# PSUM banks of nine Q blocks, the place of PQ's scaling, and the place and bank of gb's ones matmul

## Chip, core and metric

The kernel runs on one core of a Trainium2 chip. Times are device microseconds (us) of one launch. Most launches of one kernel agree within some tenths of a per cent (six of before lie within 840.26 to 841.36 us, 0.13%); every comparison of times is made with launches of the same rounds on the same chip. A profile is one such launch. The rounds ran on different chips (the medians of before were 840.96 us on chip 10, 840.87 on chip 2 and 840.8 on chip 6), so figures read from traces are compared across chips.

Five engines work side by side: TensorE (PE: matmuls; PEld: its weight loads), VectorE (DVE), ScalarE (ACT), GpSimd (POOL) and the DMA queue that SyncE (SP) feeds (in before PE was busy for 831.1, PEld for 383.5, DVE for 511.4, ACT for 336.3 and POOL for 36.3 us of the same 839.8). Matmul results go to PSUM, of which this kernel uses eight banks (0 to 7); its semaphores let a bank be written again only when the last reader is done.

## The reference, cut to what matters

```python
h = layernorm(x) * (1 + ca) + sa
q, k, v = split(h @ wqkv)                  # 2048 rows, 1024 columns, 32 heads
pq, pk = phi(q), phi(k)                    # phi(t) = max(t, 0) + min(exp(t), 1) + 1e-6, in effect
kv, z = sum pk*v, sum pk                   # per head, over all rows
o = (pq @ kv) / (pq @ z + 1e-6)            # "den" is pq @ z
x = x + ga * (o @ wo)
h = layernorm(x) * (1 + cb) + sb
x = x + gb * ((gelu(h @ w_gate) * (h @ w_up)) @ w_down)
# sa, ca, ga, sb, cb, gb: six rows of silu(c) @ w_mod
```

The first stretch that matters lies where k and v are done: the last Q blocks, den, and the fold of kv into wo (W2). The second lies at the end of the FFN of the first quarter of the rows, where the row gb is summed and spread to all partitions.

## The kernel before: the parts that matter

A helper records every operation with what it reads and writes, and turns the overlaps into semaphore waits; each engine then runs its own operations in the order of recording (in before DVE waited 0.79 us for rb, though an evacuation stood behind in its queue). So the order of the calls below is the order in each engine's queue.

A Q block is eight matmuls of 128x512 into one bank, and its evacuation is three instructions: exp on ACT, then two on DVE.

```python
def phi(bank, dst_ap, dst_rng, note):              # L669, L670, L672
    ACT: EB = exp(PS(bank))
    DVE: EB = min(EB, 1) + 1e-6
    DVE: dst = max(PS(bank), 0) + EB               # the last reader of the bank
```

den multiplies PQ with z, and its evacuation and the reciprocal follow on DVE; the reciprocal goes out to memory and comes back, spread over the partitions, as rb (sixteen loads). `pq_scale` multiplies PQ by rb on DVE, in place.

```python
q_todo += [(NSG - 1, qc) for qc in range(NG)]
qn = [0]

def q_next(evac=True):
    sg, qc = q_todo.pop(0)
    b = (0, 1, 2, 0)[qn[0]] if qn[0] < 4 else (qn[0] + 1) % 2
    qn[0] += 1
    q_block(sg, qc, evac, b)
    return sg, qc, b

first_q = q_next(False)
kvacc(NCH - 1)
zcols()
q_evac(*first_q)
q_next()
den(0, 3)                  # 32 small matmuls into bank 3; on DVE: +1e-6, reciprocal; store
rb_load(0)
rb_load(1)
kvbd()                     # DVE: three instructions, reads banks 5 to 7
q_next()
q_next()                   # the fourth Q block
for u in range(NG):
    q_next()
    if u == 0:
        kvt()              # eight transposes into bank 4
    else:
        w2_pair(u - 1)     # two matmuls into banks 2 and 3, copied by ACT
    if u in (2, 3):
        pq_scale(0, 0, GH[u - 2])
    if u in (5, 6):
        pq_scale(0, 1, GH[u - 5])
w2_pair(NG - 1, 4)
```

So the twelve Q blocks go to banks 0, 1, 2, 0, and then 1, 0, 1, 0, 1, 0, 1, 0. I number them from 1.

gb is summed on DVE in the first FFN, split in two bf16 parts (`gb_hi` on ACT, `gb_lo` on DVE), summed over the partitions by four matmuls with a matrix of ones, copied by ACT, stored and loaded back over all partitions:

```python
def gb_rows():
    mod_rows(((0, 2, 6, lambda j, h: (HLG[:, j, h, :], r_hlg(j, h))),))   # 4 matmuls 32x512, bank 6 (L643)
    o_ = mod_store(2, 6, MRG, [...], 2)                                   # ACT copy (L649), store
    row_load(GBB, R_GBB, 2, 0, "gbb", o_)

for fc, fn in ((14, lambda: gb_hi(0)), (16, lambda: gb_lo(0)), (24, lambda: gb_hi(1)), (25, lambda: gb_lo(1)), (26, gb_rows)):
    gb_at.setdefault(fc, []).append(fn)     # called after FFN column block fc of the first group
...                                         # fc runs 0 to 27; then the down projection, banks 6, 7, 4, 5, ...
```

## Time and profile before

| | before |
|---|---|
| time, median of the first 3 launches | 841.0 us (840.83 to 841.36) |
| PE busy | 831.1 of 839.8 us |
| from the third Q block to the first Wo matmul | 22.70 us |
| hole around the ones matmuls of gb | 1.48 us |

The page's first parts. Line one is the span; the PE and DVE lines are busy time, share and number of instructions; PEclk is the granted clock in tenths, in 40 slices.

```profile
span 839.8 us, 11286 instructions
...
PE 831.1 (99%) x4160; PEld 383.5 (46%) x4160; DVE 511.4 (61%) x893; ACT 336.3 (40%) x555; POOL 36.3 (4%) x91
...
PEclk9999999999999999999999999999999999999999
```

Matmuls fill the span, at full clock (mean granted clock 1.000). What can still be gained without taking work away is where PE waits. All its waits, from the view of waits for PE (engine, line, waited for: us in total, times, longest):

```profile
PE ps_all L478 <- DMA c<-in_c_dram: 2.7, 1, 2.7
PE ps_all L600 <- DMA wmq<-in_w_mod_dram: 1.2, 1, 1.2
PE ps_all L721 <- DVE pq L672: 1.1, 2, 0.7
PE ps_all L680 <- DVE h1T L565: 0.6, 2, 0.4
PE ps_all L643 <- DVE hlg L1176: 0.5, 1, 0.5
```

The first, second and fourth belong to the first 27 us and are not touched. The third and the last are the targets. PE's timeline (start, duration, line, operation, in brackets the idle time and what ended it) shows where they lie. First the Q stretch:

```profile
176.18 5.35 PE L721 MATMUL ps_all<-h1T,wq 128*128 128x512 bf16 x24
181.37 0.61 PE L940 MATMUL ps_all<-ident,kvbd 128*128 128x128 bf16 x8
182.72 1.89 PE L721 MATMUL ps_all<-h1T,wq 128*128 128x512 bf16 x8 [0.74 <-DVE pq L672]
...
190.92 0.59 PE L947 MATMUL ps_all<-wo,kvt 128*128 128x512 bf16 x2
191.85 1.90 PE L721 MATMUL ps_all<-h1T,wq 128*128 128x512 bf16 x8 [0.34 <-DVE pq L672]
193.59 0.59 PE L947 MATMUL ps_all<-wo,kvt 128*128 128x512 bf16 x2
194.12 1.90 PE L721 MATMUL ps_all<-h1T,wq 128*128 128x512 bf16 x8
...
198.88 3.62 PE L1045 MATMUL ps_all<-w,pq 128*128 128x512 bf16 x16
```

An entry's duration includes the pipelined tail of its last matmul (one full matmul is recorded with 0.38 us, and the next starts 0.22 after it: 348.03 and 348.25 below), so holes are best measured from starts. A full matmul starts 0.216 us after the one before it (see the FFN lines below), a block of eight 1.73 us after. The transposes of 181.37 are issued by 181.82, and the next block starts at 182.72: 0.9 us of nothing, though the table of waits says 0.74. Two W2 matmuls take 0.43; so 191.85 comes 0.5 us late and 194.12 about 0.1. DVE's timeline shows why:

```profile
177.50 1.75 DVE L965 RECIPROCAL rdc<-rdc 128x256 f32<-128x256 f32 x1
179.17 1.29 DVE L934 TENSOR_TENSOR kvbd<-ps_all,bmask 128x384 bf16<-128x384 f32 x3
...
181.88 0.69 DVE L672 SCALAR_TENSOR_TENSOR pq<-ps_all,eb 128x512 bf16<-128x512 f32 x1
...
189.44 1.29 DVE L991 TENSOR_TENSOR pq<-pq,rb 128x512 bf16<-128x512 bf16 x2 [0.79 <-DMA rb<-scr_rd]
190.65 0.42 DVE L670 TENSOR_SCALAR eb<-eb 128x512 f32<-128x512 f32 x1
191.11 0.69 DVE L672 SCALAR_TENSOR_TENSOR pq<-ps_all,eb 128x512 bf16<-128x512 f32 x1
```

The entry at 181.88 is the last reader of the fourth block's bank 0, and ends at 182.57; it comes late because reciprocal (1.75) and kvbd (1.29) stand ahead of it. The block at 182.72 (the sixth) rewrites bank 0. The entry at 189.44 is the scaling: it waits 0.79 us for rb, and the evacuation at 191.11 stands behind it; the block at 191.85 needs that bank.

Second, the ones matmuls (L643), between FFN column blocks 26 and 27 (L1102 and L1105):

```profile
348.03 0.38 PE L1102 MATMUL ps_all<-h2T,wg 128*128 128x512 bf16 x1
348.25 0.38 PE L1105 MATMUL ps_all<-h2T,wu 128*128 128x512 bf16 x1
348.55 0.60 PE L643 MATMUL ps_all<-hlg,ones 128*32 128x512 bf16 x3
349.62 0.39 PE L643 MATMUL ps_all<-hlg,ones 128*32 128x512 bf16 x1 [0.47 <-DVE hlg L1176]
349.95 0.39 PE L1102 MATMUL ps_all<-h2T,wg 128*128 128x512 bf16 x1
```

PE would go on at 348.25 + 0.216 = 348.47; it goes on with full matmuls at 349.95, after a hole of 1.48 us, in which the fourth ones matmul waits for `gb_lo(1)` on DVE (hlg).

### The profile page before, as it was taken

The numbers are of one execution on the slowest core, as the hardware profiler recorded it, in microseconds if no ns is written. First come the engines' busy times: TensorE is split into PE (matmuls) and PEld (weight loads), VectorE is DVE, ScalarE is ACT, GpSimd is POOL, SyncE is SP. The second block draws the span as 40 slices with busy tenths as digits, with TensorE's granted clock in tenths as the row PEclk, the third lists the DMA queues.
The fourth block names the chain that finished last, engine by engine and source line by source line (L and its number), as shares of the span: only waits on it lengthen the run. The fifth ranks groups of instructions, "written<-read, shape, count | busy, mean of one in ns | idle before, by whom it ended". The sixth has DMA issues, their size and how long they took to land.

```text
span 839.8 us, 11286 instructions
## 1 busy us (share of the span) xinstructions
PE 831.1 (99%) x4160; PEld 383.5 (46%) x4160; DVE 511.4 (61%) x893; ACT 336.3 (40%) x555; POOL 36.3 (4%) x91
## 2 busy tenths in 40 slices
PE   7999999999999999999999999999999999999998
PEld 4444444444444444444444444444444444444444
DVE  6678877687686567654456665356666535665512
ACT  2357777436413354420354442044444204444300
POOL 2011111000200000010000001000000000000000
PEclk9999999999999999999999999999999999999999
DMA  9983322239797669270555533055553305555000
GB/s 285 317 251 96 106 76 76 77 81 233 145 215 218 210 202 276 70 164 26 148 155 153 153 100 69 26 157 151 151 150 101 76 20 157 152 152 147 7 19 26
DMA packets 183942, 113.22 MB, mean 135 GB/s; under 512 B 35400, under 2 KB 174920, under 8 KB 182864
## 3 DMA queue, kind: packets, MB, share of 16 engines
q1 hardware_dynamic: 183872, 112.50, 49.8%
q8 instruction: 33, 0.54, 0.3%
q14 instruction: 21, 0.17, 0.1%
q10 hardware_dynamic: 16, 0.00, 0.0%
HBM read 100.67 MB, written 4.47 MB: 125 GB/s over the span
## 4 chain that ended last, share of the span: by engine, by line
PE 97%; DVE 1%; DMA 1%; issue 0%; ACT 0%; SPq 0%; ACTq 0%
PE ps_all L1130 23%; PE ps_all L1102 23%; PE ps_all L1105 23%; PE ps_all L680 13%; PE ps_all L1045 7%; PE ps_all L721 6%; DMA wmq<-in_w_mod_dram 1%; PE ps_all L702 1%; PE ps_all L600 0%; PE ps_all L947 0%; PE ps_all L959 0%; DVE pq L672 0%; SPq L442 0%; PE ps_all L643 0%; DVE kvbd L934 0%
## 5 line engine op out<-in xcount | busy, mean ns | idle before, releaser
L1102 PE MATMUL ps_all<-h2T,wg 128*128 128x512 bf16 x896 | 339.6, 379 | 0.0
L1105 PE MATMUL ps_all<-h2T,wu 128*128 128x512 bf16 x896 | 339.6, 379 | 0.0
L1130 PE MATMUL ps_all<-wd,yT 128*128 128x512 bf16 (+2 forms) x924 | 194.1, 373 | 0.0
L1113 ACT ACTIVATE q<-ps_all 128x512 f32<-128x512 f32 x112 | 66.9, 597 | 228.1 <-PE ps_all L1102 224.3
L1130 PEld LDWEIGHTS ps_all<-wd,yT 128*128 128x128 bf16 x924 | 89.3, 98 | 104.5
L1102 PEld LDWEIGHTS ps_all<-h2T,wg 128*128 128x128 bf16 x896 | 87.7, 98 | 105.9 <-issue 0.4
L1105 PEld LDWEIGHTS ps_all<-h2T,wu 128*128 128x128 bf16 x896 | 87.7, 98 | 105.5
L1115 DVE SCALAR_TENSOR_TENSOR ww<-q,ps_all 128x512 f32<-128x512 f32 x112 | 77.0, 687 | 78.9 <-ACT guh L1114 78.9
L1118 DVE SCALAR_TENSOR_TENSOR ww<-th,guh 128x512 f32<-128x512 f32 x112 | 77.6, 693 | 77.9 <-ACT th L1117 77.9
L1117 ACT ACTIVATE th<-ww 128x512 f32<-128x512 f32 x112 | 70.5, 629 | 87.4 <-DVE ww L1115 87.4
L1135 DVE TENSOR_TENSOR ps_all<-ps_all,gbb 128x512 f32<-128x512 f32 (+2 forms) x33 | 22.5, 683 | 94.5 <-PE ps_all L1130 94.5
L1120 DVE TENSOR_TENSOR yT<-ww,ps_all 128x512 bf16<-128x512 f32 x112 | 76.9, 687 | 3.8
L1114 ACT ACTIVATE guh<-ps_all 128x512 f32<-128x512 f32 x112 | 66.3, 592 | 0.0
L721 PE MATMUL ps_all<-h1T,wq 128*128 128x512 bf16 x256 | 58.7, 379 | 1.1 <-DVE pq L672 1.1
L680 PE MATMUL ps_all<-wk,h1T 128*128 128x512 bf16 x256 | 58.2, 379 | 0.6 <-DVE h1T L565 0.6
L680 PE MATMUL ps_all<-wv,h1T 128*128 128x512 bf16 x256 | 57.7, 379 | 0.0
L669 ACT ACTIVATE eb<-ps_all 128x512 f32<-128x512 f32 x64 | 37.4, 599 | 50.2 <-PE ps_all L721 22.9
L1045 PE MATMUL ps_all<-w,pq 128*128 128x512 bf16 x256 | 56.2, 379 | 0.0
L670 DVE TENSOR_SCALAR eb<-eb 128x512 f32<-128x512 f32 x64 | 27.1, 423 | 26.5 <-ACT eb L669 26.2
L1045 PEld LDWEIGHTS ps_all<-w,pq 128*128 128x128 bf16 x256 | 25.0, 98 | 30.2 <-issue 0.2
L680 PEld LDWEIGHTS ps_all<-wk,h1T 128*128 128x128 bf16 x256 | 24.5, 98 | 30.8 <-DVE h1T L565 2.3
L680 PEld LDWEIGHTS ps_all<-wv,h1T 128*128 128x128 bf16 x256 | 24.9, 98 | 29.8
(94 smaller groups left out, 477.3 us busy)
## 6 DMA issues: line engine op xcount, KB each, us to landing
wg<-in_B_w_gate_dram SPq DMA_DIRECT2D x56, 512.0 KB, 4.2
wu<-in_B_w_up_dram SPq DMA_DIRECT2D x56, 512.0 KB, 5.3
rb<-scr_rd SPq DMA_DIRECT2D x32, 256.0 KB, 7.5
wd<-in_B_w_down_dram SPq DMA_DIRECT2D x7, 1024.0 KB, 8.9
wmst<-in_w_mod_dram SPq DMA_DIRECT2D x6, 1024.0 KB, 6.8
wmq<-in_w_mod_dram SPq DMA_DIRECT2D x8, 512.0 KB, 7.6
out_dram<-xall SPq DMA_DIRECT2D x31, 128.0 KB, 1.7
xall<-in_A_x_dram SPq DMA_DIRECT2D x3, 1024.0 KB, 12.0
```

The costliest lines, as they stand in the source:

```text
L680: o = sch.op(T, lambda e, dc=dc: e.matmul(PS(bank), H1[sg][:, dc, ci * P:(ci + 1) * P], W_[:, dc, jg * 512:(jg + 1) * 512], start=(dc == 0 ...
L721: o = sch.op(T, lambda e, dc=dc: e.matmul(PS(b), WQ[:, dc, qc * P:(qc + 1) * P], H1[sg][:, dc, :], start=(dc == 0), stop=(dc == NDC - 1)), ...
L1045: last[half] = sch.op(T, lambda e, g=g, half=half: e.matmul(PS(b0 + half), PQ[sg][:, g, ci * P:(ci + 1) * P], W2[:, g, half * 512:(half + ...
L1102: og = sch.op(T, lambda e, dc=dc: e.matmul(PS(bg), WG[slot][:, dc, e_ * P:(e_ + 1) * P], H2[sg][:, dc, :], start=(dc == 0), stop=(dc == ND ...
L1105: ou = sch.op(T, lambda e, dc=dc: e.matmul(PS(bu), WU[slot][:, dc, e_ * P:(e_ + 1) * P], H2[sg][:, dc, :], start=(dc == 0), stop=(dc == ND ...
L1113: sch.op(A, lambda e: e.activation(Q1[j][:, :], PS(bg), ACTF.Square, scale=math.sqrt(GELU_A)), prd=pr(bg), wr=rq, note=f"q1 {fc}")
L1114: ogh = sch.op(A, lambda e: e.activation(GUH[j][:, :], PS(bg), ACTF.Copy, scale=0.5), prd=pr(bg), wr=rg, note=f"gh {fc}")
L1115: sch.op(V, lambda e: e.scalar_tensor_tensor(WW[j][:, :], Q1[j][:, :], 1.0, PS(bg), op0=ALU.add, op1=ALU.mult), rd=rq, prd=pr(bg), wr=rw, ...
L1117: sch.op(A, lambda e: e.activation(TH[j][:, :], WW[j][:, :], ACTF.Tanh, scale=GELU_C), rd=rw, wr=rt, note=f"th {fc}")
L1118: sch.op(V, lambda e: e.scalar_tensor_tensor(WW[j][:, :], TH[j][:, :], 1.0, GUH[j][:, :], op0=ALU.add, op1=ALU.mult), rd=rt + rg, wr=rw, n ...
L1120: sch.op(V, lambda e: e.tensor_tensor(YT[:, fc, :], WW[j][:, :], PS(bu), ALU.mult), rd=rw, prd=pr(bu), wr=r_yt(fc), note=f"yT {fc}")
L1130: o = sch.op(T, lambda e, b=b, fc=fc, c0=c0, c1=c1, n=n: e.matmul(PS(b, 0, n), YT[:, fc, ci * P:(ci + 1) * P], WDT[fc // 4][:, fc % 4, c0:c1],
```

## The change

Its intent: take away the two waits. The fourth Q block goes to bank 3, which den has left, and the eight later ones alternate from bank 0 on instead of bank 1 (0, 1, 0, 1, ...), so that nine of the twelve blocks change their bank and the later ones find banks 0 and 1 evacuated earlier; the scaling of PQ moves behind one more block's evacuation in DVE's queue; the ones matmuls move behind the last FFN column block, where hlg is long done. There bank 6 would be rewritten at once by the down projection, so they go to bank 7.

```diff
-            b = (0, 1, 2, 0)[qn[0]] if qn[0] < 4 else (qn[0] + 1) % 2
+            b = (0, 1, 2, 3)[qn[0]] if qn[0] < 4 else qn[0] % 2
...
-            if u in (2, 3):
-                pq_scale(0, 0, GH[u - 2])
-            if u in (5, 6):
-                pq_scale(0, 1, GH[u - 5])
+            if u in (3, 4):
+                pq_scale(0, 0, GH[u - 3])
+            if u in (6, 7):
+                pq_scale(0, 1, GH[u - 6])
...
-            mod_rows(((0, 2, 6, lambda j, h: (HLG[:, j, h, :], r_hlg(j, h))),))
-            o_ = mod_store(2, 6, MRG, [(OFF_GAB, OFF_GAB + 2048, "mrg")], 2)
+            mod_rows(((0, 2, 7, lambda j, h: (HLG[:, j, h, :], r_hlg(j, h))),))
+            o_ = mod_store(2, 7, MRG, [(OFF_GAB, OFF_GAB + 2048, "mrg")], 2)
...
-        for fc, fn in (..., (25, lambda: gb_lo(1)), (26, gb_rows)):
+        for fc, fn in (..., (25, lambda: gb_lo(1)), (27, gb_rows)):
```

More of the change, by code (lines that the diff above doesn't have):

```diff
@@ L1188, in bass_adaLN_cond__linear_attn_block__geglu_ffn__prompt_kernel @@
                 gb_at.setdefault(6 * n + 3 + k - (n == 3), []).append(lambda j=j, d=4 * q + k: gb_acc(j, d))
-        for fc, fn in ((14, lambda: gb_hi(0)), (16, lambda: gb_lo(0)), (24, lambda: gb_hi(1)), (25, lambda: gb_lo(1)), (26, gb_rows)):
+        for fc, fn in ((14, lambda: gb_hi(0)), (16, lambda: gb_lo(0)), (24, lambda: gb_hi(1)), (25, lambda: gb_lo(1)), (27, gb_rows)):
             gb_at.setdefault(fc, []).append(fn)
```

## The prediction

> **What bounds the kernel now.** TensorE. The page gives PE 831.1 of 839.8 us busy (99%), PEclk at its top digit in all 40 slices, and the chain of waits runs through PE for 97% of the span. The table of waits for PE has five entries, 6.1 us together. Three lie at the start and are not touched. The change aims at the other two: Q blocks waiting for DVE's evacuation (L721 <- DVE pq L672, 1.1 us) and the ones matmul of gb (L643 <- DVE hlg L1176, 0.5 us).
>
> **First place (176 to 199 us).** Ten Q blocks (1.727 us each, from starts 1.73 apart), eight transposes (0.45) and sixteen W2 matmuls (0.216 each, 3.45) should take 21.17 us; from 176.18 to the first Wo matmul at 198.88 they take 22.70. So 1.53 us is idle. The PE timeline puts it before the block at 182.72 (0.89 from the end of the transposes' issue) and those at 191.85 (0.5) and 194.12 (0.1).
> - The block at 182.72 rewrites bank 0, in which the fourth block is; that evacuation ends only at 182.57, because DVE runs it behind the reciprocal (1.75 us) and kvbd (1.29). After the change the fourth block goes to bank 3 (den's; its reader ends at 177.46, the block starts at 177.91) and the later ones alternate, so this block waits for the one evacuated at 177.13: no wait. The fourth block's bank is next taken by W2 at about 183.55, after 182.57.
> - The 191.85 wait: scaling of PQ stood ahead of that evacuation in DVE's queue and waited itself for its rb load (0.79 idle). One block later the data is there; by my replay of the three queues each later block finds its bank free 0.2 to 0.5 us ahead. These margins are thin.
> Saving 1.5 us.
>
> **Second place (348 to 350 us).** Four ones matmuls stand between fc 26 and 27; the last waits for glo1, which ends at 349.57. The hole between two FFN matmuls is 1.48 us (348.47 to 349.95). The same form at 153 us, unwaited, shows 12 matmuls in 1.07 us, i.e. four rounds of 0.216 plus 0.2 around them; so two rounds cost about 0.63 here. [...] One fc later glo1 is long done. Bank 7 is next written by the down projection's second half, 6 us later, so ACT's copy (0.58) doesn't hold it up; bank 6 would be needed at once. gb's row lands later, near 361 us, about when DVE first multiplies by it; that multiplication has banks with 12 us of slack.
> Saving 0.85 us.
>
> **Sum.** Both lie wholly on the critical path, and no work is added: 841.0 - 2.4 = 838.6 us, 0.3% faster. I give 838.6, range 837.8 to 839.8; faster by over 2% 0.005, within 2% 0.99, slower by over 2% 0.005.
>
> **What will show it.** Waits for PE: both entries gone, only the start's left. First Wo matmul near 197.4 instead of 198.88. L643's four matmuls in one piece after fc 27, the hole 0.6 instead of 1.5 us, PE busy share up slightly, everything later shifted by 2.4 us.
>
> **What would make it wrong.** A thin margin at a later Q block (DVE takes 2.26 us per block with scaling against PE's 2.16) brings 0.1 to 0.5 us back. The fourth block could wait for den's reader if DVE is late. [...] A different chip could move the base by some tenths.

The four rounds of the second place can be read from the starts in the trace of before: the twelve matmuls start four at a time at 153.30 to 153.33 and 153.53 to 153.55 us, and two at a time at 153.75 and 153.96 to 153.97.

## The result, and the profile after

| | before | after |
|---|---|---|
| median | 841.09 us (840.26 to 841.36, 6 launches) | 839.11 us (838.08 to 839.3, 6 launches) |
| third Q block to first Wo matmul | 22.70 us | 21.18 us |
| hole around the ones matmuls | 1.48 us | 0.63 us |
| span of the profiled launch | 839.8 us | 837.3 us |

The ratio is 0.9976, with a 95% interval of 0.9963 to 0.9988: within 2%, but clearly faster. (A ratio is the mean time of one kernel's fast launches over that of the other's of the same rounds, so not quite the ratio of the medians.) The answer was checked against the reference and correct.

The waits for PE after the change:

```profile
PE ps_all L478 <- POOL bmask L429: 2.2, 1, 2.2
PE ps_all L600 <- DMA wmq<-in_w_mod_dram: 1.3, 1, 1.3
PE ps_all L680 <- DVE h1T L565: 0.8, 2, 0.4
PE ps_all L680 <- issue: 0.4, 1, 0.4
```

Both targets are gone; what is left lies at the start. (The "issue" entry is new and 0.4 us; I did not trace it, as some 79 matmul records are missing from this trace: the page counts 4081 matmuls where before had 4160. For the same reason the page's PE busy time, 825.8 us, is lower although PE waits less, and its chain of waits strays to DMA. Neither can be compared here.)

The Q stretch on PE after the change, the same places as before:

```profile
176.09 5.35 PE L721 MATMUL ps_all<-h1T,wq 128*128 128x512 bf16 x23
181.28 0.61 PE L940 MATMUL ps_all<-ident,kvbd 128*128 128x128 bf16 x8
181.73 1.89 PE L721 MATMUL ps_all<-h1T,wq 128*128 128x512 bf16 x8
...
190.37 1.89 PE L721 MATMUL ps_all<-h1T,wq 128*128 128x512 bf16 x8
...
197.27 3.62 PE L1045 MATMUL ps_all<-w,pq 128*128 128x512 bf16 x15
```

The sixth block starts at 181.73, when the transposes are issued, and neither it nor any other entry of this stretch has an idle note. 197.27 - 176.09 = 21.18 us, against 198.88 - 176.18 = 22.70: 1.52 us less. DVE after the change, around the scaling:

```profile
189.12 0.69 DVE L672 SCALAR_TENSOR_TENSOR pq<-ps_all,eb 128x512 bf16<-128x512 f32 x1
189.73 1.28 DVE L991 TENSOR_TENSOR pq<-pq,rb 128x512 bf16<-128x512 bf16 x2
```

The scaling now starts at 189.73 without a wait, behind the evacuation of 189.12. And the ones matmuls, at the end of the FFN:

```profile
350.10 0.38 PE L1105 MATMUL ps_all<-h2T,wu 128*128 128x512 bf16 x1
350.40 0.61 PE L643 MATMUL ps_all<-hlg,ones 128*32 128x512 bf16 x4
350.95 5.35 PE L1130 MATMUL ps_all<-wd,yT 128*128 128x512 bf16 x23
```

They run in one piece, and the down projection starts 350.95 - (350.10 + 0.216) = 0.63 us late. 1.48 - 0.63 = 0.85 us less. 1.52 + 0.85 = 2.37; the spans of the two profiled launches differ by 2.5, and 0.1 of that was there before the Q stretch (175.19 against 175.10 for the first den matmul).

### The profile page after: what moved, and what is told of

It reads as the page before. It is cut to its first block, busy times and chain, and to the rows that moved or that the text cites. A ratio compares the mean times of both kernels' runs of the same rounds, so it can differ in the third digit from the quotient of the medians. Undisturbed runs are those within 1.5% of the kernel's fastest.

```text
span 837.3 us, 11206 instructions
## 1 busy us (share of the span) xinstructions
PE 825.8 (99%) x4081; PEld 383.3 (46%) x4160; DVE 511.5 (61%) x893; ACT 336.1 (40%) x555; POOL 37.1 (4%) x91
## 4 chain that ended last, share of the span: by engine, by line
PE 91%; DMA 4%; ACT 1%; DVE 1%; SPq 1%; issue 1%; POOL 0%; ACTq 0%; POOLq 0%
PE ps_all L1130 23%; PE ps_all L1105 23%; PE ps_all L1102 21%; PE ps_all L680 13%; PE ps_all L721 7%; PE ps_all L1045 2%; DMA wu<-in_B_w_up_dram 1%; DMA h2T<-xh 1%; PE ps_all L702 1%; DMA wmq<-in_w_mod_dram 1%; DMA scr_rd<-rdc 1%; DMA rb<-scr_rd 1%; SPq L978 0%; PE ps_all L947 0%; PE ps_all L600 0%
## 5 line engine op out<-in xcount | busy, mean ns | idle before, releaser
L1102 PE MATMUL ps_all<-h2T,wg 128*128 128x512 bf16 x860 | 325.9, 379 | 0.0
L721 PE MATMUL ps_all<-h1T,wq 128*128 128x512 bf16 x243 | 56.2, 379 | 0.7
```

The lines of the kernel that those rows point to most:

```text
L721: o = sch.op(T, lambda e, dc=dc: e.matmul(PS(b), WQ[:, dc, qc * P:(qc + 1) * P], H1[sg][:, dc, :], start=(dc == 0), stop=(dc == NDC - 1)), ...
L1102: og = sch.op(T, lambda e, dc=dc: e.matmul(PS(bg), WG[slot][:, dc, e_ * P:(e_ + 1) * P], H2[sg][:, dc, :], start=(dc == 0), stop=(dc == ND ...
```

## The experiments

Two theories stood against each other. Mine: PE is the only thing that counts, each hole has one cause, and the Q stretch's two edits need each other, because the scaling pins a later block to the landing of rb. The rival: the parts simply add up, or the gain is partly noise of the start or something else.

The start of a launch varies by more than the effects: the first den matmul comes between 173.89 and 175.19 us in the traces below, and not by kernel. So beside the times I give each trace's span from den's start to the end (the trace's span less the start of the first L959 matmul, before rounding), in which the start drops out.

| run | Q stretch, us | ones hole, us | den to end, us | less before | time, median us | ratio |
|---|---|---|---|---|---|---|
| before | 22.70 | 1.48 | 664.6 | | 841.0 | |
| after (first profile) | 21.18 | 0.63 | 662.2 | -2.4 | 839.11 | 0.9976 |
| whole_again | 21.18 | 0.64 | 662.2 | -2.4 | 838.26 | 0.9966 |
| banks_only | 22.73 | 1.48 | 664.6 | 0.0 | 841.0 | 1.0003 |
| scale_only | 22.09 | 1.48 | 664.0 | -0.6 | 840.41 | 0.9994 |
| gb_only | 22.51 | 0.63 | 663.5 | -1.0 | 839.98 | 0.999 |
| banks_no_dma_wait | 21.18 | 1.48 | 663.1 | -1.5 | 839.49 | 0.9981 |
| three_banks | 21.18 | 1.48 | 663.1 | -1.5 | 839.36 | 0.9986 |
| three_banks_gb | 21.18 | 0.63 | 662.2 | -2.4 | 838.62 | 0.9972 |
| gb_bank7_at26 | 23.14 | 1.48 | 665.0 | +0.4 | 841.59 | 1.0005 |
| gb_bank6 | 22.41 | 3.04 | 667.5 | +3.0 | 843.73 | 1.0034 |
| gb_bank6_b (one look) | 22.63 | 3.04 | 666.1 | +1.5 | 842.9 | |
| gb_bank6_c (one look) | 22.46 | 3.05 | 665.9 | +1.3 | 841.97 | |

Intervals of the ratios are about 0.0013 to either side (1.1 us), so the launch times alone can't tell a part of 0.6 us from nothing. The two columns of the trace can.

### whole_again: the changed kernel once more

> The changed kernel once more, in the same rounds as its parts. Theory (two idle holes of PE are closed, 1.52 us at the Q blocks and 0.84 us at the ones matmul): 2.4 us less than before, ratio 0.9972, and the same intervals within the trace as in its first profile. Rival (part of the measured 2.0 us is start-up noise between launches): the time difference moves by some tenths of a us from the first measurement while the two intervals in the trace stay the same to 0.05 us.

Edit: none against the changed kernel. Median 838.26 against 840.96, ratio 0.9966 (0.9954 to 0.9979). The first measurement had 2.0 us between the medians, this one 2.7; both traces have 21.18 and 0.63 to 0.64, and 662.2 us from den to the end. So 2.4 us is what the change does, and the rest of either difference is variation between launches, of which the start alone shows 175.10 against 173.89. Both statements were expected.

### banks_only: the banks without the later scaling

> Only the Q blocks' banks changed; scaling of PQ and gb as before. Theory (the scaling, which waits for its rb load until 189.4 us and stands ahead of an evacuation in DVE's queue, pins the later block): the hole of 0.9 us before the block at 182.72 is gone, but the block that started at 191.85 still starts at 191.8 to 191.9, behind a hole grown from 0.5 to about 1.4 us. Saving in all 0 to 0.2 us: time within 0.3 us of before. Rival (the parts add up, each hole belongs to its own edit): 0.9 us less than before.

```diff
-            b = (0, 1, 2, 0)[qn[0]] if qn[0] < 4 else (qn[0] + 1) % 2
+            b = (0, 1, 2, 3)[qn[0]] if qn[0] < 4 else qn[0] % 2
```

Median 841.0 against 840.96: nothing. PE and DVE around the later block:

```profile
181.51 1.89 PE L721 MATMUL ps_all<-h1T,wq 128*128 128x512 bf16 x8
...
189.71 0.59 PE L947 MATMUL ps_all<-wo,kvt 128*128 128x512 bf16 x2
191.58 1.90 PE L721 MATMUL ps_all<-h1T,wq 128*128 128x512 bf16 x8 [1.27 <-DVE pq L672]
```

```profile
186.75 0.69 DVE L672 SCALAR_TENSOR_TENSOR pq<-ps_all,eb 128x512 bf16<-128x512 f32 x1
189.16 1.29 DVE L991 TENSOR_TENSOR pq<-pq,rb 128x512 bf16<-128x512 bf16 x2 [1.73 <-DMA rb<-scr_rd]
190.37 0.42 DVE L670 TENSOR_SCALAR eb<-eb 128x512 f32<-128x512 f32 x1
190.83 0.69 DVE L672 SCALAR_TENSOR_TENSOR pq<-ps_all,eb 128x512 bf16<-128x512 f32 x1
```

The sixth block has no hole any more (181.51 follows on the transposes), and all 0.9 us come back before the block at 191.58. (I had expected it at 191.8 to 191.9; this launch's Q stretch began 0.31 us earlier, at 175.87, and from there it is 15.71 us against 15.67 in before.) PE had gained 0.9 us, DVE's scaling then waited 1.73 us for rb instead of 0.79, and the evacuation at 190.83 was as late as ever. My theory's reading held, and "the parts add up" fell.

### scale_only: the later scaling without the banks

> Only the scaling of PQ one block later; banks and gb as before. Theory: the hole before the block at 182.72 stays (0.9 us), the holes at 191.85 and 194.12 (0.5 and 0.1) go: first Wo matmul near 198.3 instead of 198.88, 0.6 us less than before. With banks_only at 0, the two together (1.5) are more than the sum of each alone. Rival (parts add up): 0.6 as well, but then banks_only gives 0.9.

```diff
-            if u in (2, 3):
-                pq_scale(0, 0, GH[u - 2])
-            if u in (5, 6):
-                pq_scale(0, 1, GH[u - 5])
+            if u in (3, 4):
+                pq_scale(0, 0, GH[u - 3])
+            if u in (6, 7):
+                pq_scale(0, 1, GH[u - 6])
```

The stretch takes 22.09 us, 0.61 less, with the 0.9 us hole before the sixth block left. The median is 0.55 us lower, inside the noise of the launch times (ratio 0.9981 to 1.0008). Banks alone 0.0, scaling alone 0.6, both 1.5: the banks' 0.9 us is only paid out when the scaling has moved.

### banks_no_dma_wait: is it the wait for rb, or the work?

> The banks of banks_only, and the scaling in its old place, but the first four scaling instructions multiply by a tile that has long been in memory instead of by rb: same instructions, same sizes, no wait for the load (wrong result on purpose). Theory (the wait for rb, 1.73 us of DVE's idle time in banks_only, holds up the evacuation behind it): the hole of 1.3 us before the block at 191.58 goes, the stretch from the first Q block after den to the first Wo matmul takes 21.2 us instead of 22.7, about 1.5 us less than before. Rival (DVE has too much work there: 2.26 us per block with scaling against PE's 2.16): the hole stays at 0.3 us or more, and the saving is below 1.2 us.

```diff
 def pq_scale(sg, h, gs):
     ...
+        if sg == 0 and h == 0:     # same instruction, other factor: GAB, loaded long ago
+            PQ[0][:, g0:g1, 0:HW] *= GAB[:, 0:2 * HW]
+            continue
```

(on top of banks_only; cut and put in short. The real edit also makes the load that reuses this buffer wait for the first load itself, as nothing reads that any more). Its output is wrong, which doesn't matter for the time. The Q stretch takes 21.18 us, as with the whole change. DVE:

```profile
186.32 0.69 DVE L672 SCALAR_TENSOR_TENSOR pq<-ps_all,eb 128x512 bf16<-128x512 f32 x1
186.93 1.28 DVE L990 TENSOR_TENSOR pq<-pq,gab 128x512 bf16<-128x512 bf16 x2
188.13 0.42 DVE L670 TENSOR_SCALAR eb<-eb 128x512 f32<-128x512 f32 x1
```

The same scaling in the old place runs at once, and no Q block waits. So the work of the scaling (DVE's 2.26 us per block) was not the cause, the wait for rb was. From the end of the reciprocal (start 177.50 plus 1.75 before) to the landing of rb it takes 189.44 - 179.25 = 10.2 us in before; 10.0 in gb_only and 10.6 in gb_bank7_at26. That variation is what makes the Q stretch of the kernels with the old scaling and two alternating banks differ (22.41 to 23.14 us) without any edit there: in all six traces of them with the old banks, and in banks_only, the stretch less this time is 12.50 to 12.52 us. So it is the landing of rb that sets the length of the stretch, and freeing only the fourth block's bank can't shorten it.

### three_banks: more banks instead of a later scaling

> Scaling in its old place and still waiting for rb; the fourth Q block in bank 3, and the later ones go round three banks (0, 1, 5) instead of two: each rewrites the bank of the block three earlier. Theory (the late evacuation holds PE only because the bank comes round after two blocks): DVE still waits about 1.7 us for rb, but PE doesn't wait; 21.2 us for the stretch, about 1.5 us less than before. Rival (scaling has to be moved, whatever the banks): a hole of 1 us or more stays before some later block, saving below 0.5 us.

```diff
-            b = (0, 1, 2, 0)[qn[0]] if qn[0] < 4 else (qn[0] + 1) % 2
+            b = (0, 1, 2, 3)[qn[0]] if qn[0] < 4 else (0, 1, 5)[(qn[0] - 4) % 3]
```

The Q stretch takes 21.18 us, with the scaling in its old place. DVE waits for rb about as long as in banks_only (1.84 us, 1.73 there):

```profile
188.91 1.29 DVE L991 TENSOR_TENSOR pq<-pq,rb 128x512 bf16<-128x512 bf16 x2 [1.84 <-DMA rb<-scr_rd]
```

DVE is as late as there, and PE doesn't notice. So the later scaling isn't needed where a bank comes round after three blocks instead of two. Two banks were enough where no evacuation stood behind the wait for rb (21.18 us in the changed kernel), too few where one did (22.73 us in banks_only, with 1.73 us of waiting), and three were enough where a DMA held one up by 1.84 us.

### three_banks_gb: does the other way beat the change?

> three_banks together with the move of gb's ones matmul (after fc 27, bank 7): the scaling of PQ stays in its old place. Theory (a third bank does for the Q blocks what the fourth block's bank and the later scaling do together): both holes gone, 21.2 us for the Q stretch and 0.64 for the ones matmul, span from den's start to the end 662.2 us as in the changed kernel, 2.4 us less than before; no faster than the changed kernel. Rival (the later scaling gains something of its own beyond the holes): some tenths slower than the changed kernel from den's start on.

Edit: three_banks, and the move of the ones matmuls as in the change. 21.18 us, 0.63 us, 662.2 us from den to the end; median 838.62, ratio 0.9972. The same as the change, and no faster, as expected. It doesn't depend on when rb lands, which the change does up to a point: in the changed kernel's first profile DVE reached the scaling at 189.73, 10.56 us after the end of the reciprocal, and rb had landed before that. In gb_bank7_at26 rb took 10.62 us. A landing as late as that would make DVE wait in the changed kernel too, and PE would have only the margins of 0.3 to 0.6 us that are listed below.

### gb_only: the ones matmuls alone

> Only gb's ones matmul, after fc 27 and in bank 7. Theory: the hole between the last FFN matmul and the next full matmul shrinks from 1.48 to 0.64 us, 0.84 us less than before, Q blocks as before. Rival ([...] the gain depends on the Q part's shift): another hole than 0.64, or another saving than the hole shows.

```diff
-            mod_rows(((0, 2, 6, ...
-            o_ = mod_store(2, 6, MRG, ...
+            mod_rows(((0, 2, 7, ...
+            o_ = mod_store(2, 7, MRG, ...
-        for fc, fn in (..., (26, gb_rows)):
+        for fc, fn in (..., (27, gb_rows)):
```

The hole is 0.63 us, 0.85 less. Den to end is 1.0 less; the other 0.2 is the Q stretch, in which rb landed 0.2 us earlier. The median of the launches is 1.0 us lower (ratio 0.9978 to 1.0003).

### gb_bank7_at26: the bank alone

> Only the bank of gb's ones matmul changed to 7, still after fc 26. Theory (the wait there is for glo1 on DVE, not for a bank): the hole stays at 1.48 us with its wait for hlg of about 0.5, time within 0.3 us of before. Rival (something holds bank 6): the hole shrinks to 0.64.

Only the two bank numbers of gb_only's edit. The hole is 1.48 us, with its wait for hlg of 0.5: bank 6 held nothing up in the old place. The median was 0.7 us above before (ratio 1.0005, 0.9993 to 1.0018), more than the 0.3 that I had allowed; in the trace 0.4 us is in the Q stretch (rb landed 10.6 us after the reciprocal), which this edit doesn't touch, and the ones hole is the same.

### gb_bank6, and two more looks at it: the place alone

> Only the place of gb's ones matmul moved (after fc 27), still in bank 6. Theory (the down projection's first matmul rewrites bank 6 and must wait for ACT's copy, which stands behind fc 27's tanh in ACT's queue): the hole from the last FFN matmul to the first down matmul is about 3.1 us (from before: tanh of fc 27 ends 2.5 us after the last FFN matmul, the copy takes 0.6), against 0.64 in gb_only: 1.6 us slower than before. Rival (the bank doesn't matter, only the place does): 0.64, and 0.84 us faster than before.

Only `(26, gb_rows)` to `(27, gb_rows)`. The wait for PE that this makes:

```profile
PE ps_all L1130 <- ACT mrg L649: 2.3, 1, 2.3
```

The down projection's first matmul waits for ACT's copy out of bank 6, behind the tanh of column block 27. The hole is 3.04 us where I expected 3.1, and the rival fell. But the time was 2.9 us over before (843.73 against 840.87 in the medians), not 1.6. The view of stretches shows the rest (window, its length, busy time and instructions of PE, PEld, DVE, ACT, POOL, then PE's granted clock, DMA share, GB/s):

```profile
351.00:354.00 3.00, 0.65 (x5) 0.11 (x2) 1.65 (x3) 2.00 (x4) 0.00 (x0) 1.00 0.00 0
354.00:356.00 2.00, 2.00 (x8) 0.83 (x7) 1.93 (x3) 0.00 (x0) 0.00 (x0) 0.70 0.01 2
356.00:358.00 2.00, 2.00 (x7) 0.62 (x5) 1.18 (x5) 0.59 (x1) 0.55 (x1) 0.50 0.76 162
358.00:360.00 2.00, 1.95 (x9) 0.89 (x9) 1.22 (x4) 0.66 (x2) 0.55 (x1) 0.94 0.94 236
360.00:362.00 2.00, 2.00 (x11) 0.90 (x10) 0.18 (x1) 1.24 (x1) 0.00 (x0) 1.00 1.17 324
```

After the restart at 353.81 the clock was 0.70, 0.50 and 0.94 of full in three stretches of 2 us: 0.60 + 1.00 + 0.12 = 1.7 us of work lost, as much as the middle stretch's 0.50 would lose in 3.4 us. If it was 0.50 throughout, the outer stretches put it from 354.8 to 358.2 us, an estimate (1.2 us before 356 and 0.24 after 358).

> gb_bank6 looked at a second time. It was 2.9 us slower than before where the hole (3.05 us against 1.48) gives 1.6; its trace shows the granted clock at 0.5 for 3.4 us, starting 1.0 us after PE's restart. Theory (the long hole brings the clock down[...]): the hole is 3.05 us again, and the half clock comes again near the hole with another start, or doesn't come; with it the time is near 844, without it near 842.5. Rival (the half clock was chance, without a link to the hole): no half clock at all near 351 to 358 us, and 842.5.

> gb_bank6 looked at a third time, as the one before: hole 3.05 us; half clock of 3.4 us near it, or none, and the time goes with it by about 1.7 us (half of 3.4).

Both have the same hole (3.04 and 3.05 us), and full clock around it (1.00 in every stretch from 340 to 362 us). From den to the end, without the Q stretch, they take 666.1 - 22.63 = 643.5 and 665.9 - 22.46 = 643.4 us; the first took 667.5 - 22.41 = 645.1. So the clock cost 1.7 us, as the stretches say. By the mean clock that each launch lists (0.998 instead of 1.0), four of the five timed launches had such a loss (843.66 to 844.97 us) and the fifth didn't (842.67); with the two, that is four of seven. Only one of the four has a trace that shows where it was, so for the other three the place is inferred.

What decides whether the clock falls is not shown. PE's wait was the same 2.35 us in all three traces (351.46 to 353.81 in gb_bank6, 352.41 to 354.75 in gb_bank6_b, 351.46 to 353.81 in gb_bank6_c), and the clock fell after it in the first alone.

Elsewhere the mean clock 0.998 occurs in 4 of 52 launches of the kernels that have the 1.48 us hole (before in these rounds, banks_only, scale_only, banks_no_dma_wait, three_banks, gb_bank7_at26) and in none of 21 of the kernels in which it is 0.63. The 1.48 us hole could have brought it, but that one has only some 0.5 us of waiting, less than the 2.35 us after which the clock stayed full in gb_bank6_b and gb_bank6_c. None of these four launches is the profiled one, and 0 of 21 against 4 of 52 can be chance; it stays open.

## Why the prediction was right

It gave 838.6 us, within 837.8 to 839.8; the two measurements of the change are 839.11 and 838.26.

- "Saving 1.5 us" at the Q blocks: 1.52, and 1.52 again. Shown to be the banks and the scaling together by banks_only (0.0) and scale_only (0.6). The prediction had given 0.9 to the banks and 0.6 to the scaling as if the holes were separate; it didn't say that the first without the second is worth nothing. The sum was right because both were made.
- The cause of the later hole, the scaling's wait for rb ahead of an evacuation: shown by banks_no_dma_wait, where the same work without the wait leaves no hole.
- The thin margins: "0.2 to 0.5 us". From the trace after, the last DVE evacuation instruction of the block two earlier ends 0.3 to 0.6 us before each block from the seventh on starts (at 189.12 + 0.69 = 189.81 for the block at 190.37). None was used up.
- "Saving 0.85 us" at the ones matmuls: 0.85, shown by gb_only. The estimate of 0.63 for the group without a wait came from a longer group of the same form in the trace of before, and measured 0.63. The trace after puts the 0.2 us around two rounds of 0.216 where the form of the matmuls changes: its four start two by two, at 350.41 and 350.63, the first of the group starts 0.31 us after the last full matmul and the first full one 0.31 us after the group's last pair, 0.09 to 0.10 over 0.216 each. No run here isolates what causes it.
- "Bank 6 would be needed at once": gb_bank6, 3.04 us of hole.
- First Wo matmul "near 197.4": 197.27. Busy share "up slightly": can't be read, records are missing.
- gb's row "near 361 us": its load was issued at 355.04 and took 4.2 us, so 359.2. That is 1.8 us earlier than predicted; which step of the estimate was too late isn't on record. It mattered to nothing: DVE's first multiplication by it started at 359.43, 0.2 us later.

## What to carry to other kernels

When one engine is busy 99% of the time, list its waits, measure each hole from starts (not from the table of waits, which said 1.1 and 0.5 us for 1.52 and 0.85), and ask for each which one instruction of which engine ended it. A hole that is closed early in a pipeline comes back at the next place that is pinned to something else, here a DMA landing (0.9 us closed in banks_only, and 1.27 us of waiting at a later block), so look for the next pin before you count the gain; one more buffer in the rotation can make the other edit needless (the later scaling: 21.18 us in three_banks without it). Keep an instruction that may wait for a DMA out of the queue ahead of one that frees a buffer, and remember that a hole of TensorE can cost more than its length (here 1.7 us on top of one of 3.04, in one of three traces).
